# First weight loads of an expert layer: released by one memset on GpSimd in place of four on VectorE

## The chip, the cores and the metric

The kernel runs on one core of a Trainium2 chip. The metric is the device time of one execution in microseconds, the median of the runs. The engines go by the profile's names where rows are shown: PE is TensorE (PEld its weight loads), DVE is VectorE, ACT is ScalarE, POOL is GpSimd and SP is SyncE, which here only issues transfers. A small q behind a name (POOLq, SPq) is that engine's sequencer.

## The reference

A layer with a convolution gated by a query comes first, and a switch layer with eight experts after it. Only the second matters here:

```python
def _B_ref(x, w_gate, w1, w2):          # x: layernorm(h), 2048 rows of 512
    logits = xf @ w_gate                # 8 experts
    topk_idx = jnp.argsort(-logits, axis=-1)[:, :1]
    gates = _softmax(topk_val, axis=-1)
    for e in range(8):
        w = (gates * (topk_idx == e)).sum(-1, keepdims=True)
        out = out + w * (_silu(xf @ w1[e]) @ w2[e])   # w1[e]: 512 x 1792, w2[e]: 1792 x 512
h2 = h + _B_ref(_layernorm(h), ...)
```

Each token goes to one expert. All is float32.

## The kernel before

The first part (to line 611) computes the convolution and writes h, 2048 rows of 512, to a buffer in DRAM, `h_dram`. A routing part (lines 613 to 771) finds each token's expert, counts the tokens of each, picks the expert with the fewest as the first, and makes the list `idx0` of its rows. Every engine then branches on `wide_i`, a flag made from the counts, to one of three copies of `experts` (line 1037 loads it and line 1038 branches); the profiled execution takes the one with the capacities `SNUG`, in which the first expert has 240 places, two tiles of 128 and 112 rows.

Ahead of the branch, GpSimd gathers the rows of the first expert from `h_dram` in two indirect DMAs, one for each tile (line 762, tiles `rows0`, which the profile shows as part of `kt`), and SP loads the first two chunks of its weights, `raw0` (line 769). A chunk is 128x1024 numbers, 512 KB; an expert has 14, seven of w1 and seven of w2. Two memsets on GpSimd (line 781) clear `end1` and `end2`, which are used at the very end.

Inside `experts`, the order on each engine is the order in which the program writes the instructions. The float32 products are made in three passes from a high and a low part: `split_hi` copies a chunk to `whi` on ScalarE (line 877), `split_lo` subtracts on VectorE to `wlo` (line 882). `norm` (line 846, VectorE) normalises a tile of rows, `turn_x` transposes it on TensorE (line 855), copies to `xh` on ScalarE (line 856) and makes `xl` on VectorE (line 857). `up` multiplies with w1 (line 900), takes SiLU on ScalarE into one of three buffers `s` (line 903), casts to `hh` on VectorE (line 904) and subtracts to `hl` on GpSimd (line 905). `down` multiplies with w2 (lines 921 and 924). Rows of the next expert are gathered on GpSimd (line 833) while the present one is computed, and their norm and transposes stand in the middle of the present expert's `down`.

`load_w` (line 859) loads chunk s on SP: chunks 0 and 1 are `raw0`, and the following ones go to six buffers `raw` (line 869). Eight chunks are loaded ahead (`AHEAD`), and four are split ahead (`LEAD`). From chunk 8 on a load waits until `split_lo` has done with the buffer's old chunk. With `after` set, `load_w` first writes one column of the buffer, and the load has to wait for that write; the value is overwritten by the load. In the kernel before, this is done for chunks 2 to 5, on VectorE, in a place behind the norm of the first tile and a first half of `split_lo(0)`; the loads of chunks 6 and 7 stand behind them in SP's queue.

After the loads, TensorE runs through all chunks: `up` for seven, `down` for seven, expert by expert.

Of the kernel before, what the change touches and what calls it, by code (L numbers as in the profile page):

```python
# [7 lines left out]
F32 = mybir.dt.float32  # L8
# [9 lines left out]
P = 128  # L18
S, D, F, E, KS = 2048, 512, 1792, 8, 4
# [112 lines left out]
def kernel(  # L132
# [3 lines left out]
    nc = tc.nc  # L136
# [339 lines left out]
    PACE, ZERO, AHEAD = 5.404, 26.722, 1.943  # L476
# [24 lines left out]
    for n in range(ND):  # L501
        b = 4 * (n - 1)
        z, f = (b + B0, F0 * BU) if n == 0 else (b, BU)
# [37 lines left out]
        for u in range(NU):  # L541
# [11 lines left out]
            for kind, d in (("k", DA[1]), ("u", DA[2])):  # L553
                for r in range(2):
                    first = u == 0 and r == 0
# [23 lines left out]
        for u in range(NU):  # L579
            o = 4 * c + 4 + FO[c] + FS[c] * u  # L580
# [177 lines left out]
            nc.vector.tensor_reduce(perm_i, eqe, axis=AX.X, op=ALU.add)  # L758

    first = ctx.enter_context(tc.tile_pool(name="first", bufs=1))  # L760
    for t in range(2):
        nc.gpsimd.indirect_dma_start(
            out=rows0[t], out_offset=None, in_=h_dram[:, :],
            in_offset=bass.IndirectOffsetOnAxis(ap=idx0[:, t:t + 1], axis=0))
    place0 = nc.sync.value_load(least[0:1], min_val=0, max_val=E - 1)
    raw0 = []
    for ch in range(2):
        raw = first.tile([P, 1024], F32, name=f"raw{ch}")
# [7 lines left out]
    half_i = small([2], "half_i", I32)  # L776
    end = 3 * ORDER[-1] + 1
    halves = out.rearrange("s (i d) -> (s i) d", i=2)
    ends = [first.tile([P, D], F32, name="end0")] + [first.tile([P, D // 2], F32, name=f"end{i + 1}") for i in range(2)]
    for o in ends[1:]:  # L780
        nc.gpsimd.memset(o, 0.0)
    scat = []

    def scatter(to, at, o, n_rows):
# [20 lines left out]
    def experts(caps):  # L805
# [12 lines left out]
        LEAD, AHEAD = 4, 8  # L818
# [3 lines left out]
        def tiles(n):  # L822
            cap = caps[ORDER[n]]
            return [(t, r0, min(P, cap - r0), 3 * ORDER[n] + t) for t, r0 in enumerate(range(0, cap, P))]
# [34 lines left out]
        def load_w(s, after=False):  # L859
            if s >= 2 * NCH * E:  # L860
                return
            n, r = divmod(s, 2 * NCH)
            if s < len(raw0):
                PV[n], RAW[s] = place0, raw0[s]
                return
            if r == 0:
                PV[n] = nc.sync.value_load(perm_i[0:1, ORDER[n]:ORDER[n] + 1], min_val=0, max_val=E - 1)
            w, ch = (w1, r) if r < NCH else (w2, r - NCH)
            raw = RAW[s] = wp.tile([P, 1024], F32, name="raw")
            if after:  # L870
                nc.vector.memset(raw[:, 0:1], 0.0)
            nc.sync.dma_start(raw, w[bass.ds(PV[n], 1), ch].rearrange("o p f -> (o p) f"))

        def split_hi(s):
            whi = wp.tile([P, 1024], F32R, name="whi", bufs=8)
            wlo = wp.tile([P, 1024], F32R, name="wlo", bufs=8)
            nc.scalar.activation(whi, RAW[s], AF.Copy)  # L877
            W[s] = whi, wlo

        def split_lo(s, a=0, b=1024):  # L880
            whi, wlo = W[s]
            nc.vector.tensor_sub(wlo[:, a:b], RAW[s][:, a:b], whi[:, a:b].bitcast(F32))  # L882
# [80 lines left out]
                send(n, t, m, pd[:m], X["part"][:m, cols], None, ends[half + 1])  # L963

        firsts, last = tiles(0)[:-1], tiles(0)[-1]
        for s in range(len(raw0)):
            load_w(s)
            split_hi(s)
        marks(A_T, A_T, 24)
        ptab = ps_u.tile([P, 24], F32, name="acc")  # L970
        selected(ptab, A_T, 24, F16)
        norm(0, *firsts[0])
        split_lo(0, 0, 512)
        for s in range(len(raw0), AHEAD):
            load_w(s, s < 6)
        for a in firsts[1:]:
            norm(0, *a)
        for half in range(2):
# [15 lines left out]
        for s in range(2 * NCH * E):  # L994
            n, r = divmod(s, 2 * NCH)
            nx = tiles(n + 1) if n + 1 < E else []
            load_w(s + AHEAD)
            if 1 <= r - NCH < 1 + len(nx):
                norm(n + 1, *nx[r - NCH - 1])
# [38 lines left out]
    with tc.If(wide > 0, preferred_fallthrough_block=False) as sizes:  # L1038
        wider = nc.values_load(wide_i[0:1, 1:2], min_val=0, max_val=1, skip_runtime_bounds_check_because=flag)
        with tc.If(wider > 0) as more_sizes:  # L1040
            experts(CAPS)
        with more_sizes.Else():
            experts(TIGHT)
# [16 lines left out]
        with tc.If(more > 0):  # L1060
# [33 lines left out]
            for e in range(E):  # L1094
# [3 lines left out]
                with tc.For_i(min(CAPS) // P, nt) as t:  # L1098
# [29 lines left out]
                    for ch in range(NCH):  # L1128
# [3 lines left out]
                        for i in range(2):  # L1132
                            f = 2 * ch + i
                            nc.tensor.matmul(py, ht[:, f, :], wr[:, i, :], start=f == 0, stop=f == 2 * NCH - 1)
                    o = g2p.tile([P, D], F32, name="go")
# [6 lines left out]
    with sizes.Else():  # L1142
        experts(SNUG)
# [79 lines left out]
```

## Time and profile before

| | us |
|---|---|
| median of 3 runs | 543.25 (541.98 to 543.84) |
| the profiled execution, its time | 543.93 |
| its span, from the first to the last instruction | 542.0 |
| TensorE busy | 521.0 (96% of the span) |
| VectorE busy | 391.8 (72%) |
| GpSimd busy | 279.1 (52%) |
| ScalarE busy | 264.6 (49%) |

The busy times are unions over the span. Times in the rows count from the start of the span, and the stage of the change lies from about 184 to 235 us. Busy shares of the whole span say little about that stage; the timelines and the chain of waits do.

### The profile page before, as it was taken

How to read it: one execution, taken by the hardware profiler on the slowest of the kernel's cores; microseconds unless marked ns; L12 is line 12 of the kernel's file. 1: busy time of each engine (PE TensorE's matmuls, PEld its weight loads, DVE VectorE, ACT ScalarE, POOL GpSimd, SP SyncE). 2: the span in 40 equal slices, each digit the busy share in tenths (PEclk: the TensorE clock that was granted, in tenths of full speed). 3: DMA queues.
4: the chain of work that ended last, by engine and by line, in shares of the span. 5: the costliest groups of instructions: out<-in, count | busy, mean ns of one | idle time of the engine just before them, and what ended most of it. 6: DMA issues, size and time to landing. Idle time of an engine off the chain costs nothing.

```text
span 542.0 us, 12326 instructions
## 1 busy us (share of the span) xinstructions
PE 521.0 (96%) x4875; PEld 455.3 (84%) x4875; DVE 391.8 (72%) x556; ACT 264.6 (49%) x410; POOL 279.1 (52%) x324
## 2 busy tenths in 40 slices
PE   8999989999998989999999999999999999999994
PEld 8967777767656879689999999999988988988973
DVE  3779899898997979679655775864856765765851
ACT  2787887534321346545435444555544644554520
POOL 0455649865653237828703841850870850851832
PEclk9999999999999999999999999999999999999998
DMA  8919686659651378675554565665658557666401
GB/s 280 393 47 282 224 276 187 191 144 303 182 159 52 95 241 302 199 271 179 172 195 145 194 186 186 202 207 183 200 171 285 182 174 264 199 189 232 155 2 39
DMA packets 41156, 105.26 MB, mean 194 GB/s; under 512 B 5174, under 2 KB 13496, under 8 KB 40706
## 3 DMA queue, kind: packets, MB, share of 16 engines
q1 hardware_dynamic: 37682, 95.89, 53.9%
q0 software_dynamic: 3408, 8.51, 4.8%
q8 instruction: 40, 0.66, 0.5%
q14 instruction: 26, 0.21, 0.1%
HBM read 95.96 MB, written 8.50 MB: 193 GB/s over the span
## 4 chain that ended last, share of the span: by engine, by line
PE 80%; DVE 6%; issue 4%; DMA 4%; ACT 3%; POOL 1%; SPq 1%; POOLq 0%; DVEq 0%
PE acc L900 30%; PE acc L921 15%; PE acc L924 12%; PE pa L295 8%; PE pb L331 7%; PE pa L367 5%; DMA kt<-in_kt_dram 3%; PE pm L279 2%; PE pt L855 1%; DVE xa L344 1%; DVE zs L352 1%; DMA kt<-h_dram,idx 1%; PE pt L944 1%; DVE bst L381 1%; ACT ac L263 1%
## 5 line engine op out<-in xcount | busy, mean ns | idle before, releaser
L882 DVE TENSOR_TENSOR wlo<-raw,whi 128x1024 fp32r<-128x1024 f32 (+1 forms) x113 | 155.4, 1385 | 36.3 <-ACT whi L877 36.1
L905 POOL TENSOR_TENSOR hl<-s,hh 128x240 fp32r<-128x240 f32 (+5 forms) x112 | 102.8, 935 | 135.9 <-DVE hh L904 135.3
L877 ACT ACTIVATE whi<-raw 128x1024 fp32r<-128x1024 f32 x112 | 114.6, 1052 | 7.4 <-DMA raw<-in_w_dram 3.1
L903 ACT ACTIVATE s<-acc 128x240 f32<-128x240 f32 (+5 forms) x112 | 43.1, 387 | 113.0 <-PE acc L900 62.2
L904 DVE CAST hh<-s 128x240 fp32r<-128x240 f32 (+5 forms) x112 | 47.3, 430 | 54.4 <-ACT s L903 54.2
L900 PE MATMUL acc<-xh,whi 128*128 128x240 f32 (+5 forms) x448 | 72.6, 285 | 0.2 <-ACT xh L856 0.2
L900 PE MATMUL acc<-xl,whi 128*128 128x240 f32 (+5 forms) x448 | 71.8, 283 | 0.0
L900 PE MATMUL acc<-xh,wlo 128*128 128x240 f32 (+5 forms) x448 | 71.8, 283 | 0.0
L900 PEld LDWEIGHTS acc<-xh,whi 128*128 128x128 f32 x448 | 61.6, 189 | 0.9 <-ACT xh L856 0.4
L900 PEld LDWEIGHTS acc<-xl,whi 128*128 128x128 f32 x448 | 61.4, 189 | 0.0
L900 PEld LDWEIGHTS acc<-xh,wlo 128*128 128x128 f32 x448 | 61.3, 189 | 0.0
L921 PE MATMUL acc<-whi,hh 128*128 128x512 f32 (+2 forms) x136 | 54.4, 400 | 0.0
L921 PE MATMUL acc<-whi,hl 128*128 128x512 f32 (+2 forms) x136 | 53.7, 395 | 0.0
L921 PE MATMUL acc<-wlo,hh 128*128 128x512 f32 (+2 forms) x136 | 53.4, 393 | 0.0
L267 POOL TENSOR_TENSOR acc<-acc,ac 128x512 f32<-128x512 f32 x26 | 33.1, 1282 | 36.7 <-ACT acc L255 18.3
L924 PE MATMUL acc<-hh,whi 128*128 128x304 f32 (+2 forms) x168 | 49.7, 296 | 0.0
L924 PE MATMUL acc<-hl,whi 128*128 128x304 f32 (+2 forms) x168 | 49.2, 293 | 0.0
L924 PE MATMUL acc<-hh,wlo 128*128 128x304 f32 (+2 forms) x168 | 49.2, 293 | 0.0
L298 ACT ACTIVATE st<-pa 128x512 f32<-128x512 f32 x64 | 37.3, 595 | 19.6 <-PE pa L295 19.2
L295 PEld LDWEIGHTS pa<-kv,tw 128*128 128x128 f32 x256 | 30.2, 191 | 12.2 <-ACT st L298 8.7
L295 PE MATMUL pa<-kv,tw 128*128 128x128 f32 x256 | 33.5, 282 | 2.2 <-ACT st L298 2.2
L924 PEld LDWEIGHTS acc<-hh,whi 128*128 128x128 f32 x168 | 31.6, 188 | 0.1
(196 smaller groups left out, 892.4 us busy)
## 6 DMA issues: line engine op xcount, KB each, us to landing
raw<-in_w_dram SPq DMA_DIRECT2D x112, 512.0 KB, 4.2
tv<-in_tab_v_dram SPq DMA_DIRECT2D x12, 512.0 KB, 4.3
h<-in_q_dram SPq DMA_DIRECT2D x16, 256.0 KB, 5.1
kt<-in_kt_dram SPq DMA_DIRECT2D x3, 1216.0 KB, 8.0
v<-in_v_dram SPq DMA_DIRECT2D x12, 256.0 KB, 4.4
kern<-in_ssm_dram SPq DMA_DIRECT2D x12, 256.0 KB, 3.7
h<-in_x_dram SPq DMA_DIRECT2D x12, 256.0 KB, 3.5
h_dram<-h SPq DMA_DIRECT2D x12, 256.0 KB, 4.1
```

The lines of the kernel that those rows point to most:

```text
L267: nc.gpsimd.tensor_add(T[a, c, u], T[a, c, u], T[b, c, u])
L295: nc.tensor.matmul(p[:, :, j], tw[:, u * UJ + j, r, :], src[:, j, :], start=True, stop=True)
L298: nc.scalar.activation(T["s" + kind, c][:, r * NU + u], T["pa", kind, c, u, r], AF.Copy)
L331: nc.tensor.matmul(out[b, g, :], w[a], x[a, g, :], start=n == 0, stop=n == len(parts) - 1)
L877: nc.scalar.activation(whi, RAW[s], AF.Copy)
L882: nc.vector.tensor_sub(wlo[:, a:b], RAW[s][:, a:b], whi[:, a:b].bitcast(F32))
L900: nc.tensor.matmul(pu, a[:, k, at], b[:, k, :], start=i == k == 0, stop=i == 2 and k == ND - 1)
L903: nc.scalar.activation(s, pu, AF.Silu)
L904: nc.vector.tensor_copy(hh[:, f, :], s)
L905: nc.gpsimd.tensor_sub(hl[:, f, :], s, hh[:, f, :].bitcast(F32))
L921: nc.tensor.matmul(pd[:ds_.stop - ds_.start], b[:, f, ds_], a[:, f % 2, :], start=f == 0 and i == 0, stop=f == last - 1 and i == 2)
L924: nc.tensor.matmul(pd, a[:, f % 2, ds_], b[:, f, :], start=f == 0 and i == 0, stop=f == 2 * NCH - 1 and i == 2)
```

## The change

Chunks 2 to 7 are now all loaded ahead of the splits. Only the load of chunk 2 is preceded by a write to its buffer, and this write is now on GpSimd, where it stands behind the two gathers of the first expert's rows in that engine's order. Chunks 3 to 7 have no such write and follow in SP's order. The two memsets of `end1` and `end2` and the buffers themselves are moved ahead of the gathers. Nothing is computed otherwise than before.

```diff
@@ -758,6 +758,9 @@
             nc.vector.tensor_reduce(perm_i, eqe, axis=AX.X, op=ALU.add)
 
     first = ctx.enter_context(tc.tile_pool(name="first", bufs=1))
+    ends = [first.tile([P, D], F32, name="end0")] + [first.tile([P, D // 2], F32, name=f"end{i + 1}") for i in range(2)]
+    for o in ends[1:]:
+        nc.gpsimd.memset(o, 0.0)
     for t in range(2):
         nc.gpsimd.indirect_dma_start(
             out=rows0[t], out_offset=None, in_=h_dram[:, :],
@@ -776,9 +779,6 @@
     half_i = small([2], "half_i", I32)
     end = 3 * ORDER[-1] + 1
     halves = out.rearrange("s (i d) -> (s i) d", i=2)
-    ends = [first.tile([P, D], F32, name="end0")] + [first.tile([P, D // 2], F32, name=f"end{i + 1}") for i in range(2)]
-    for o in ends[1:]:
-        nc.gpsimd.memset(o, 0.0)
     scat = []
 
     def scatter(to, at, o, n_rows):
@@ -868,7 +868,7 @@
             w, ch = (w1, r) if r < NCH else (w2, r - NCH)
             raw = RAW[s] = wp.tile([P, 1024], F32, name="raw")
             if after:
-                nc.vector.memset(raw[:, 0:1], 0.0)
+                nc.gpsimd.memset(raw[:, 0:1], 0.0)
             nc.sync.dma_start(raw, w[bass.ds(PV[n], 1), ch].rearrange("o p f -> (o p) f"))
 
         def split_hi(s):
@@ -963,16 +963,15 @@
                 send(n, t, m, pd[:m], X["part"][:m, cols], None, ends[half + 1])
 
         firsts, last = tiles(0)[:-1], tiles(0)[-1]
+        for s in range(AHEAD):
+            load_w(s, s == len(raw0))
         for s in range(len(raw0)):
-            load_w(s)
             split_hi(s)
         marks(A_T, A_T, 24)
         ptab = ps_u.tile([P, 24], F32, name="acc")
         selected(ptab, A_T, 24, F16)
         norm(0, *firsts[0])
         split_lo(0, 0, 512)
-        for s in range(len(raw0), AHEAD):
-            load_w(s, s < 6)
         for a in firsts[1:]:
             norm(0, *a)
         for half in range(2):
```

## Rows read from the trace of the kernel before

**Rows 1.** This is the profile's page, its part in 40 equal slices of the span: the TensorE clock that was granted, in tenths of full speed.

```profile
PEclk9999999999999999999999999999999999999998
```

**Rows 2.** This is the timeline of TensorE, 184 to 236 us: start, duration, line, operation, tiles, shapes, count, and in brackets the idle time ahead of it and what ended that.

```profile
194.56 0.63 PE L855 MATMUL pt<-cs,xr 128*128 128x128 f32 x4 [1.50 <-DVE xr L846]
...
196.50 1.19 PE L900 MATMUL acc<-xh,whi 128*128 128x240 f32 x8 [0.22 <-ACT xh L856]
...
226.55 0.66 PE L855 MATMUL pt<-cs,xr 128*128 128x128 f32 x4 [1.14 <-DVE xr L846]
```

**Rows 3.** This is busy time by stretches: start and end, length, then for each engine the busy time and the number of instructions, the granted clock of TensorE, the DMA engines' share, GB/s.

```profile
196.50:225.40 28.90, 28.90 (x210) 26.46 (x210) 21.75 (x36) 15.13 (x27) 19.62 (x23) 1.00 0.85 290
...
226.60:533.50 306.90, 306.90 (x2171) 288.08 (x2172) 204.29 (x251) 143.79 (x226) 151.79 (x149) 1.00 0.56 186
...
538.00:540.00 2.00, 0.00 (x0) 0.00 (x0) 0.00 (x0) 0.00 (x0) 0.00 (x0) 0.50 0.01 2
```

**Rows 4.** This is the chain of waits from 184 to 232 us: start, duration, what.

```profile
189.51 4.33 DMA kt<-h_dram,idx
...
195.19 0.67 PE acc L985 x6
...
196.50 19.20 PE acc L900 x168
...
226.00 0.51 DVE xr L846
```

**Rows 5.** This is the timeline of VectorE, 184 to 232 us, columns as in rows 2.

```profile
195.07 0.06 DVE L871 MEMSET raw<- 128x1 f32 x1
195.07 0.41 DVE L846 TENSOR_SCALAR xr<-kt,mr 112x256 f32<-112x256 f32 x1
...
202.71 1.25 DVE L882 TENSOR_TENSOR wlo<-raw,whi 128x1024 fp32r<-128x1024 f32 x1 [0.74 <-ACT whi L877]
204.37 1.23 DVE L882 TENSOR_TENSOR wlo<-raw,whi 128x1024 fp32r<-128x1024 f32 x1 [0.42 <-ACT whi L877]
205.51 0.47 DVE L904 CAST hh<-s 128x240 fp32r<-128x240 f32 x2
...
224.81 1.23 DVE L882 TENSOR_TENSOR wlo<-raw,whi 128x1024 fp32r<-128x1024 f32 x1 [0.58 <-ACT whi L877]
```

**Rows 6.** This is the timeline of ScalarE, 182 to 232 us, columns as in rows 2.

```profile
201.61 1.06 ACT L877 ACTIVATE whi<-raw 128x1024 fp32r<-128x1024 f32 x1 [1.81 <-DMA raw<-in_w_dram]
203.28 1.06 ACT L877 ACTIVATE whi<-raw 128x1024 fp32r<-128x1024 f32 x1 [0.61 <-DMA raw<-in_w_dram]
...
207.72 0.37 ACT L903 ACTIVATE s<-acc 128x240 f32<-128x240 f32 x1 [1.65 <-POOL hl L905]
...
223.46 0.37 ACT L903 ACTIVATE s<-acc 128x240 f32<-128x240 f32 x1 [2.59 <-POOL hl L905]
223.73 3.89 ACT L877 ACTIVATE whi<-raw 128x1024 fp32r<-128x1024 f32 x4
```

**Rows 7.** This is the timeline of GpSimd, 182 to 245 us, columns as in rows 2.

```profile
189.51 1.20 POOL L762 DMA_INDIRECT kt<-h_dram,idx  x1 [1.73 <-DVE wide_i L736]
191.01 0.95 POOL L762 DMA_INDIRECT kt<-h_dram,idx  x1 [0.30 <-issue]
191.96 0.58 POOL L781 MEMSET end<- 128x256 f32 x2
...
205.88 3.89 POOL L905 TENSOR_TENSOR hl<-s,hh 128x240 fp32r<-128x240 f32 x4 [1.88 <-DVE hh L904]
...
218.55 1.37 POOL L905 TENSOR_TENSOR hl<-s,hh 128x240 fp32r<-128x240 f32 x2
...
222.72 1.37 POOL L905 TENSOR_TENSOR hl<-s,hh 128x240 fp32r<-128x240 f32 x2
```

**Rows 8.** This is the instructions of line 1038 (the branch on wide_i) from 189 to 192 us, one on each sequencer: count, shortest, median and longest duration in ns, first and last start in us.

```profile
L1038 POOLq COMPARE_BRANCH  x1: 40/40/40, 190.2 to 190.2; - x1
L1038 SPq COMPARE_BRANCH  x1: 53/53/53, 190.7 to 190.7; - x1
```

**Rows 9.** This is what SP's DMA queue waited for, 190 to 200 us: the line, what ended the wait, us in total, times, the longest.

```profile
SPq L872 <- DVE xr L846: 4.5, 1, 4.5
```

**Rows 10.** This is busy time by stretches around the gathers of the first expert, and one where the gathers of the next one run; columns as in rows 3.

```profile
192.50:193.00 0.50, 0.50 (x9) 0.46 (x8) 0.00 (x0) 0.50 (x1) 0.04 (x1) 1.00 0.56 123
...
193.50:194.00 0.50, 0.00 (x0) 0.00 (x0) 0.13 (x1) 0.00 (x0) 0.00 (x0) 1.00 0.70 270
...
194.50:195.00 0.50, 0.44 (x4) 0.47 (x5) 0.50 (x1) 0.00 (x0) 0.00 (x0) 1.00 0.00 0
...
195.50:196.00 0.50, 0.50 (x7) 0.48 (x6) 0.50 (x2) 0.32 (x1) 0.00 (x0) 1.00 0.00 0
196.00:196.50 0.50, 0.28 (x4) 0.07 (x2) 0.50 (x2) 0.41 (x2) 0.00 (x0) 1.00 0.63 131
196.50:197.00 0.50, 0.50 (x4) 0.50 (x5) 0.50 (x2) 0.28 (x2) 0.00 (x0) 1.00 0.95 270
...
217.00:218.00 1.00, 1.00 (x6) 0.80 (x5) 0.70 (x2) 0.00 (x0) 0.69 (x2) 1.00 0.84 266
```

**Rows 11.** This is DMA issues by line in the stretch 190.95 to 191.5 us, which holds the second gather of the first expert alone: count, and the median us from issue to landing.

```profile
kt<-h_dram,idx POOLq DMA_INDIRECT x1, 3.8
```

**Rows 12.** This is the same for 216.1 to 217.3 us, which holds the first gather of the next expert alone.

```profile
hr<-h_dram,idxg POOLq DMA_INDIRECT x1, 5.6
```

## The prediction

> **What bounds the kernel now.** I read the page first. TensorE's granted clock stays at its upper level until the last slice [rows 1], and the engine is busy for 521 of 542 us. So only its own idle time can be given back, and the next view is its timeline, with the idle time ahead of an instruction in brackets: transposes of normalised rows waited 1.50 us for VectorE's norm at 194.56 and 1.14 at 226.55, and the first matmul of the experts 0.22 for a ScalarE copy [rows 2]. By stretches, TensorE has no gap from 196.5 to 225.4 and none from 226.6 to 533.5 [rows 3]. The expert phase therefore has two weak places: the wait for the first rows ahead of 196.5, and one hole from 226.55 - 1.14 = 225.41 on.
>
> The chain of waits says how the first comes about [rows 4]. The first gather is issued at 189.51 and lands 4.33 later, norm, transposes, three warming matmuls (195.19 + 0.67 = 195.86), ScalarE's copy, and the first matmul at 196.50. The weights for it (raw 0 and 1) are loaded elsewhere and the edit leaves them alone. So the six loads that are moved are not on this chain.
>
> The second place hangs on GpSimd. The hole ends when VectorE has done the norm for expert 1 (226.00 + 0.51) [rows 4]. Going back from there: VectorE's split of chunk 11 at 224.81 [rows 5] waits for ScalarE's copy at 223.73, which stands behind a SiLU copy at 223.46 that waited 2.59 us for GpSimd's hl (three buffers of s) [rows 6]. GpSimd runs from 205.88 to that hl at 222.72 with hl and the gathers of expert 1 [rows 7]. It starts at 205.88 because VectorE casts the first hh only at 205.51, after the splits of chunks 2, 3 and 4; two of these were preceded by idle time, 0.74 and 0.42 us, both for ScalarE [rows 5], and ScalarE had waited 1.81 and 0.61 us for the landing of raw [rows 6]. Thus late weights do reach TensorE, by a long way round.
>
> **The change part by part.** *The wait removed.* SP was through its branch at 190.7 and then stood 4.5 us before the first of the six loads, at 195.17 [rows 8, 9]. GpSimd's sequencer was through its branch at 190.2 [rows 8], so its memset of 128x1 can run right behind the second gather, whose issue ends at 191.01 + 0.95 = 191.96, as the memsets of 128x256 do now [rows 7]. A 128x1 memset on GpSimd isn't in the trace: below it is nothing, above it is one of 128x256, 0.33 us (two in 0.58, overlapped). I take 0.2. The loads then leave at about 192.2, 3.0 us earlier. Behind the waiting instruction on SP are only loads 3 to 7 and the ones that wait for their buffers.
>
> *What the earlier loads give.* The idle 0.74 + 0.42 on VectorE goes, since chunks 3 and 4, which ScalarE began at their landing at 201.61 and 203.28 [rows 6], then land some 3 us earlier, before VectorE comes to them. The four VectorE memsets went together at 195.07 and the next norm started at the same 195.07 [rows 5]; I put 0.05 on them (nothing to the 0.06 of the one that shows by itself). VectorE's lead at the first hh is 1.16 + 0.05 = 1.21 us. I carry it one to one along GpSimd's queue to the norm at 226.00, since the outputs of TensorE lie waiting: the SiLU copy of 207.72 also waited for hl, not for TensorE [rows 6].
>
> *The memsets of ends.* They move ahead of the two gathers, 0.58 us. GpSimd stood 1.73 us before the first gather [rows 7], which hides them; without that cover the whole 0.58 would be on the chain, at the gather. Cost: nothing. The three fewer memsets, and the loads written ahead of the splits, add nothing to any other queue.
>
> *What the earlier loads cost.* The second gather is still moving. The first load, issued at 195.17, moves nothing until 196.0 [rows 10], so one issued at 192.2 starts near 193.15. The gather's data run from 192.9 to 194.5 (123 to 270 GB/s, gone by 194.5) and nothing else is in the queues [rows 10]; its tail of 1.3 us would be shared. The price g, by which the second gather lands later: nothing, if the engines have room; above, the gather of expert 1 that was issued amid loads (DMA share 0.84 [rows 10]) took 5.6 us to land where this one took 3.8, so 1.8 [rows 11, 12]. I take 0.9, half, because here the gather has a start of 0.3 us and a load moves at half rate in its first half microsecond (131 GB/s, then 270 [rows 10]): 1.8 x (1.3 - 0.5) / 1.6 = 0.9.
>
> With g, the second tile's norm (195.07, its data there since 191.01 + 3.8 = 194.8) has a slack of 0.2, and TensorE, which is at the warming matmuls until 195.86 while the first half is ready at 195.48, another 0.4. So VectorE's lead is 1.21 - (g - 0.2), and TensorE starts g - 0.6 late. At 226.55 TensorE resumes at the later of 226.55 minus the lead and 225.41 plus the late start. g = 0.9: lead 0.51, start 0.3 late, gain 0.5. g = 0: the whole 1.14. g = 1.8: lead -0.39, a loss of 0.4.
>
> **The sum.** Gain 0.5 us (1.14 to -0.4). The profiled execution took 543.93 us (span 542.0 and 1.93 around it), 0.68 above the median of 543.25. It would take 543.4; a median of like runs 543.25 - 0.5 = 542.75, said as 542.7.
>
> The Trainium skill has a rule that speaks against this change (*DMA: Bandwidth & Descriptors*, *Queues, rings and completion order*): each DMA engine goes round robin, a packet at a time, between the queues that have work. By that rule the gather's data could at most take twice their 1.6 us, g up to 1.6 and a loss of 0.2 where the row gives up to 0.4; it leaves no place for the third rival below. The longer landing amid loads [rows 12] agrees with it.
>
> **The rivals.**
> 1. *No contention, the hole closes.* Gain 1.14: 542.1. For it: a DMA share of only 0.56 to 0.70 under the gather [rows 10]. Against it: 5.6 against 3.8 us [rows 11, 12].
> 2. *The loads leave earlier and nothing comes of it.* Either the memset is held on GpSimd, or the lead is eaten on the way: VectorE's splits and GpSimd's hl run side by side, and the four hl from 205.88 took 3.89 us where two took 1.37 later [rows 7]. Gain 0: 543.25. This is also the case that the change doesn't do what it says; against it, the branch at 190.2 [rows 8].
> 3. *Slower: the gather is held behind the loads.* The place is the second tile's norm. Six loads stand in SP's queue; two that followed each other landed 203.28 - 201.61 = 1.67 us apart [rows 6]. If the gather's rest comes only after two of them, g = 3.3, and the loss is 3.3 - 0.2 - 1.21 = 1.9: 545.2. It decides from g = 1.4 on (no gain) and is beyond a measurement of this kernel from g = 3.0 on. TensorE would then stand for over 4 us, and after it stops at 534 its granted clock is at 0.50, the lower of its two levels, by 538 [rows 3]; such a fall would come on top. Against it: even amid loads a gather landed within 5.6 us.
> 4. *More than the hole.* Faster by over 1.6 us would need idle time of TensorE that isn't there, other than the 1.5 us for the first gather, whose data are through before the loads start.
>
> **How the numbers follow.** About 0.3% (1.6 us) is what a measurement of this kernel can tell from no change; its three runs alone span 541.98 to 543.84. Forecast (542.7, contention in part): 0.60. Rival 1 (542.1): 0.15. Rival 2 (543.25): 0.12. Rival 3 (545.2): 0.08. Rival 4: 0.05. Of the first three, 0.87 together, I give 0.08 to medians that fall below 541.6 by spread alone and 0.01 to ones above: faster 0.13, same 0.78, slower 0.09. The range is 542.1 to 543.65 from the bounds of g, with the spread of the medians, about 0.9 below and 0.3 above: 541.2 to 543.9.
>
> **What would show it.** After: the first of the six loads issued at 192.0 to 192.4, behind a memset at 191.96; the second gather landing 0.2 to 1.6 us later than 3.8 from its issue; first matmul at 196.5 to 197; no idle time on VectorE before the splits of chunks 3 and 4; the first hl near 205.4; the hole at 225.4 down from 1.14 to a few tenths. Wrong if the first matmul is later than 197.5, or the hole stays at 1.1 with the loads early, or a hole opens that isn't in the trace of before.

## The result, and the profile after

The changed kernel is slower: a median of 546.8 us (544.17 to 547.77, 9 runs) against 543.62 before (541.98 to 544.08, 9 runs), a ratio of 1.006 with a 95% interval of 1.004 to 1.008. Its profiled execution took 547.41 us with a span of 545.6, 3.6 longer than the span before.

What TensorE waited for from 186 to 534 us (line, what ended the wait, us in total, times, the longest), after:

```profile
PE acc L855 <- DVE xr L846: 2.2, 1, 2.2
PE pt L855 <- DVE xr L846: 0.4, 1, 0.4
```

The hole ahead of the next expert's transposes, 1.14 us in [rows 2], is gone. In its place stand 2.2 us at the transposes of the second tile (tile acc), which had no wait before. The chain of waits, 180 to 240 us, after:

```profile
190.78 6.47 DMA kt<-h_dram,idx
...
197.28 0.42 DVE xr L846
...
198.89 21.45 PE acc L900 x168
220.34 9.72 PE acc L921 x42
```

The second gather now stands on the chain, where the first stood before [rows 4]: 6.47 us from issue to landing instead of 3.8 [rows 11]. The first matmul is at 198.89 and not at 196.50, and its group of 168 takes 21.45 us and not 19.20. The granted clock, in stretches (columns as in rows 3), after:

```profile
196.50:197.00 0.50, 0.00 (x0) 0.00 (x0) 0.00 (x0) 0.00 (x0) 0.00 (x0) 1.00 0.95 246
197.00:198.85 1.85, 0.98 (x4) 0.63 (x4) 1.57 (x4) 0.36 (x1) 0.00 (x0) 0.51 0.89 308
198.85:204.00 5.15, 5.11 (x24) 5.11 (x25) 4.94 (x13) 3.64 (x6) 1.03 (x2) 0.51 0.77 311
204.00:220.00 16.00, 16.00 (x145) 16.00 (x144) 13.05 (x19) 7.78 (x15) 14.00 (x16) 1.00 0.72 238
```

TensorE has no instruction at 196.5 to 197.0, the clock falls to its lower level, and the first 24 matmuls take 5.1 us. The standing in TensorE's timeline, after:

```profile
194.77 0.83 PE L984 MATMUL acc<-cs 128*128 128x128 f32 x6
197.84 0.98 PE L855 MATMUL acc<-cs,xr 112*128 112x112 f32 x4 [2.23 <-DVE xr L846]
```

TensorE ran out of work at 194.77 + 0.83 = 195.60, and the clock fell at 197.0, 1.4 us into the standing. The account of the span: 198.89 - 196.50 = 2.39 for the late start, 21.45 - 19.20 = 2.25 for the clock, less 1.14 for the hole, together 3.50 of the 3.6 us.

What released the loads: GpSimd's and SP's timelines, after.

```profile
190.78 0.95 POOL L765 DMA_INDIRECT kt<-h_dram,idx  x1 [0.30 <-issue]
191.73 0.12 POOL L871 MEMSET raw<- 128x1 f32 x1
```

```profile
191.87 3.94 SPq L872 DMA_DIRECT2D raw<-in_w_dram  x6
```

The first load is issued 0.14 us after the gather's issue has ended (190.78 + 0.95 = 191.73). DMA packets by queue in 194.7 to 197.1 us, after (packets, MB, share of 16 engines):

```profile
q1 hardware_dynamic: 210, 0.75, 93.6%
q0 software_dynamic: 4, 0.01, 1.3%
```

Queue 0 carries the gathers, queue 1 the loads. Before, neither gathers nor loads moved from 194.5 on until the first load's data at 196.0 [rows 10]. Now a last four of the gather's packets come in this stretch among 210 of the loads, and the norm of 112 rows waits for them. The two gathers of the first expert are 160 packets of queue 0, 80 each, so it is a small part of the second gather that comes last.

### The profile page after: what moved, and what is told of

Its sections match the earlier page's. It is cut to its first block, busy times and chain, and to the rows that moved or that the text cites. A ratio compares the mean times of both kernels' runs of the same rounds, so it can differ in the third digit from the quotient of the medians.

```text
span 545.6 us, 12320 instructions
## 1 busy us (share of the span) xinstructions
PE 524.8 (96%) x4875; PEld 458.5 (84%) x4875; DVE 390.8 (72%) x552; ACT 264.4 (48%) x410; POOL 277.5 (51%) x325
## 4 chain that ended last, share of the span: by engine, by line
PE 82%; DVE 8%; issue 4%; DMA 2%; ACT 2%; POOL 1%; POOLq 0%; DVEq 0%
PE acc L900 30%; PE acc L921 15%; PE acc L924 12%; PE pa L295 8%; PE pb L331 7%; PE pa L367 4%; PE pa L459 2%; DVE xa L344 2%; PE pm L279 2%; PE pt L855 1%; DMA kt<-h_dram,idx 1%; DVE zs L352 1%; DVE p L340 1%; PE pt L944 1%; DVE bst L381 1%
## 5 line engine op out<-in xcount | busy, mean ns | idle before, releaser
L905 POOL TENSOR_TENSOR hl<-s,hh 128x240 fp32r<-128x240 f32 (+5 forms) x112 | 100.4, 914 | 138.2 <-DVE hh L904 137.7
```

What stands on the lines that cost most here:

```text
L905: nc.gpsimd.tensor_sub(hl[:, f, :], s, hh[:, f, :].bitcast(F32))
```

## The experiments

Theory A, made from this: the loads run beside the end of the second gather, it lands late, TensorE stands, and standing lowers its clock. Medians of the kernel before, measured together with each version, stand beside its result.

**Which part of the change.** `rest` puts the release back (the one memset on VectorE again, and the loads in their old place in the program) and leaves all else; `landed` keeps the place and makes the loads wait for the gather's landing.

```diff
 # rest: the loads of chunks 2 to 7 again behind split_lo(0, 0, 512)
-                nc.gpsimd.memset(raw[:, 0:1], 0.0)
+                nc.vector.memset(raw[:, 0:1], 0.0)
 ...
-        for s in range(AHEAD):
-            load_w(s, s == len(raw0))
+        for s in range(len(raw0)):
+            load_w(s)
 ...
         split_lo(0, 0, 512)
+        for s in range(len(raw0), AHEAD):
+            load_w(s, s == len(raw0))
 # landed
-                nc.gpsimd.memset(raw[:, 0:1], 0.0)
+                nc.gpsimd.tensor_copy(raw[:, 0:1], rows0[1][:, 0:1])
```

Expected of rest: 

> The changed kernel without the early release: the one memset is on VectorE again, behind the norm of the first tile; the rest of the change (one memset, not four; the memsets of ends ahead of the gathers; the buffers) stays. Theory A: the second gather lands after 3.8 us, the first matmul at 196.4, time 543.2 to 544.0, the same as before. Theory B: 546 to 547.

Expected of landed: 

> The changed kernel, but the write to chunk 2's buffer on GpSimd copies one column of the second gather's rows, so the loads wait until that gather has landed. Theory A (the six loads share the DMA engines with the second gather, it lands late, TensorE stands and its clock falls): the gather lands 3.8 us after its issue as before, the first load is issued near 194.8, the first matmul of the experts is at 196.2 to 196.6 at the upper clock, and the time is 543.0 to 543.8. Theory B (the loss comes from another part of the change: the buffers that lie elsewhere, the memsets of ends ahead of the gathers, the loads written ahead of the splits): the time stays at 546 to 547.

Measured: rest 543.85 us, ratio 1.0004 [0.9991, 1.0017]; landed 543.83, ratio 1.0005 [0.9991, 1.0020]; before 543.35. Theory B falls: the buffers that lie elsewhere, the single memset, the memsets of ends in their new place and the order of the loads cost nothing that these runs can tell. The loss is in the early release.

**The clock.** `warm` fills TensorE's time, `idle` makes TensorE stand without any early load.

```diff
 # warm, on the changed kernel
-        for _ in range(3):
+        for _ in range(12):
             nc.tensor.matmul(warm, const("one"), cs[:, :P], start=True, stop=True)
 # idle, on rest
+        for _ in range(4):
+            nc.vector.memset(ends[0], 0.0)
         for half in range(2):
             norm(0, *last, half)
```

Expected of warm: 

> The changed kernel with twelve warming matmuls in place of three between the transposes of the two tiles, so that TensorE is busy while the second gather is late. Theory A: the gather is as late as in the changed kernel (6 to 6.5 us from issue), the first matmul is still near 198.9, but the granted clock stays at its upper level, the first 168 matmuls take 19.2 us and not 21.45, and the time is 544.2 to 544.9. Theory C (the clock falls for another reason than TensorE's standing, such as the DMA traffic or where the stage happens to lie): the clock falls all the same and the time is 546.5 or more.

Expected of idle: 

> The kernel of the run rest (one memset on VectorE in the old place, so that no load is early) with four memsets of 128x512 on VectorE ahead of the norm of the second tile: about 2.2 us more of standing for TensorE, without any transfer beside the second gather. Theory A: standing alone lowers the clock. The gather lands 3.8 us after issue, the first matmul is near 198.7, part of the first 168 matmuls runs at the lower level, and the time is 545.0 to 547.0. Theory C (the clock fell because of the transfers, not because TensorE stood): the clock stays up and the time is 544.0 to 544.7, the late start less the hole of 1.1 us.

Measured: warm 544.4 us, ratio 1.0026 [1.0013, 1.0040], before 543.35; idle 547.37, ratio 1.0056 [1.0031, 1.0082], before 543.44. VectorE's timeline of warm (norm of the second tile), then TensorE's stretches of warm:

```profile
196.54 0.74 DVE L846 TENSOR_SCALAR xr<-kt,mr 112x256 f32<-112x256 f32 x2 [2.15 <-DMA kt<-h_dram,idx]
```

```profile
193.00:198.10 5.10, 4.88 (x49) 4.46 (x47) 2.80 (x6) 0.98 (x3) 0.00 (x0) 1.00 0.95 331
198.10:217.10 19.00, 18.97 (x168) 18.97 (x169) 17.97 (x30) 11.41 (x21) 12.96 (x15) 1.00 0.77 260
```

The gather is late here too (VectorE waits 2.15 us for it), but TensorE is busy meanwhile, the clock stays up and the 168 matmuls take 19.0 us. The median is 2.4 us below that of the changed kernel, which agrees with the 2.25 of its trace. Nor do transfers alone lower the clock: the DMA engines are 95% busy in the first of these stretches. TensorE's waits in idle, its stretches, a line of its chain, and the landing of its second gather in the stretch 191.9 to 195:

```profile
195.08 0.63 PE L855 MATMUL pt<-cs,xr 128*128 128x128 f32 x4 [1.63 <-DVE xr L846]
195.54 0.83 PE L988 MATMUL acc<-cs 128*128 128x128 f32 x6
198.46 0.98 PE L855 MATMUL acc<-cs,xr 112*128 112x112 f32 x4 [2.08 <-DVE xr L846]
```

```profile
196.60:203.40 6.80, 4.87 (x22) 4.55 (x23) 6.28 (x17) 2.90 (x6) 0.00 (x0) 0.50 0.92 329
203.50:220.00 16.50, 16.50 (x149) 16.50 (x149) 14.87 (x20) 9.12 (x17) 14.22 (x16) 1.00 0.79 276
```

```profile
199.51 20.88 PE acc L900 x168
```

```profile
kt<-h_dram,idx POOLq DMA_INDIRECT x1, 3.9
```

With the gather on time and TensorE standing, the clock is at its lower level for 6.8 us and the time is about that of the changed kernel. The account is the same too: 199.51 - 196.50 = 3.0 for the late start, 20.88 - 19.20 = 1.7 for the clock, less 1.14 for the hole, 3.6 in all, as the spans differ (545.6 and 542.0). The median lies above the range of theory A, and further above the 544.0 to 544.7 of theory C, which falls as far as it put the clock down to transfers: neither an early load nor a late gather is needed for this loss.

Which standing lowered the clock in idle is not shown. TensorE ran out of work at 195.54 + 0.83 = 196.37, and the clock was down from 196.6 on, 0.2 us into the added standing; another of 1.63 us had ended at 195.08. And standing isn't the only thing that the clock falls after. A stretch of rest, all that TensorE waited for in rest from 186 to 534 us, and a stretch of the changed kernel ahead of its gathers' landing:

```profile
191.60:198.30 6.70, 6.42 (x35) 4.81 (x35) 4.65 (x12) 2.88 (x6) 0.95 (x1) 0.50 0.62 193
```

```profile
PE pt L855 <- DVE xr L846: 0.2, 1, 0.2
```

```profile
192.00:192.50 0.50, 0.50 (x2) 0.02 (x1) 0.00 (x0) 0.23 (x1) 0.00 (x0) 0.50 0.57 229
```

In rest the clock was down from 191.6 to 198.3 with TensorE busy before and in it, and in the changed kernel it was down once already while TensorE ran the matmuls ahead of the first transposes. There it cost little: the first transposes came at 194.30 in the changed kernel and at 194.56 before [rows 2], and the median of rest is that of before. Why it fell there is open. What warm shows is narrower than theory A: with the gather late, keeping TensorE busy at this place kept the clock up.

**How many loads, and how early.** `early1` releases chunk 2 alone on GpSimd, the others from VectorE in the old place; `early1_again` is the same kernel; `nowait` drops the memset.

```diff
 # early1
-                nc.gpsimd.memset(raw[:, 0:1], 0.0)
+                (nc.gpsimd if s == len(raw0) else nc.vector).memset(raw[:, 0:1], 0.0)
 ...
-        for s in range(AHEAD):
+        for s in range(len(raw0) + 1):
             load_w(s, s == len(raw0))
 ...
         split_lo(0, 0, 512)
+        for s in range(len(raw0) + 1, AHEAD):
+            load_w(s, s == len(raw0) + 1)
 # nowait
-            load_w(s, s == len(raw0))
+            load_w(s)
```

Expected of early1: 

> Only chunk 2 is released early, by the memset on GpSimd; chunks 3 to 7 wait for a memset on VectorE in the old place. Theory A, with a price that grows with the bytes beside the gather: one load of 512 KB is 1.3 us of traffic, the gather lands 4.3 to 5.0 us after issue, the first matmul is at 196.5 to 197.2, time 543.0 to 544.3. Theory D (one packet of the gather on one DMA engine is held up as soon as any load is beside it): the gather is as late as with six loads, 6 us and more, and the time is 546 or more.

Expected of early1_again: 

> The same kernel as early1, for a second profile. Its runs lay apart, 542.7 to 544.4 and 545.5 to 546.2, and the profiled one was late (546.23, gather 6.1 us). If a late gather is an event of some executions, a profile near 543.5 shows the second gather landing 3.8 to 4.5 us after issue; one near 546 shows 5.5 us or more again.

Expected of nowait: 

> The changed kernel without its memset: the six loads leave as soon as SP is through its branch, near 190.9, before the second gather is issued, and move from 191.9 on, beside both gathers. Theory A (the price grows with the bytes beside the gathers): the first gather lands later too, by 0.5 to 1.5 us, the second 2.7 us late or more, the first matmul at 199.5 or later, and the time is 547 to 550. Theory D (one DMA engine's share of the gather is held up, however many loads there are): the second gather 2 to 3 us late as in the changed kernel, 546 to 547.5.

Measured: early1 543.85 us, ratio 1.0003 [0.9984, 1.0022], before 543.35, runs from 542.7 to 546.23; early1_again 544.21, ratio 1.0010 [0.9992, 1.0028], before 543.52, runs from 542.15 to 546.21; nowait 547.9, ratio 1.0078 [1.0059, 1.0098], before 543.52. The norm of the second tile on VectorE in early1, and in early1_again:

```profile
197.22 0.74 DVE L846 TENSOR_SCALAR xr<-kt,mr 112x256 f32<-112x256 f32 x2 [1.81 <-DMA kt<-h_dram,idx]
```

```profile
195.26 0.73 DVE L846 TENSOR_SCALAR xr<-kt,mr 112x256 f32<-112x256 f32 x2 [1.07 <-DMA kt<-h_dram,idx]
```

Their second gathers on GpSimd:

```profile
191.16 0.95 POOL L765 DMA_INDIRECT kt<-h_dram,idx  x1 [0.30 <-issue]
```

```profile
190.81 0.95 POOL L765 DMA_INDIRECT kt<-h_dram,idx  x1 [0.30 <-issue]
```

The gathers were issued at 191.16 and 190.81, so the norm came 6.06 and 4.45 us later, in one and the same kernel with one load released beside the gather. Queue 0 (the gathers) from 194.8 to 197.0 us in early1, and in early1_again, and a stretch of early1 in the columns of rows 3:

```profile
q0 software_dynamic: 5, 0.02, 1.8%
```

```profile
q0 software_dynamic: 1, 0.00, 0.0%
```

```profile
195.50:196.00 0.50, 0.50 (x4) 0.50 (x3) 0.00 (x0) 0.18 (x1) 0.00 (x0) 0.50 0.19 74
```

In the late execution 5 packets of the gather's 80 were still to come, a sixteenth of it, and this while the DMA engines were only 19% busy. The next load was issued at 195.5, behind VectorE's memset, so the one early load had delayed the gather before any other left. The price is thus not a fixed one for so many bytes: a single load can do what six do, and need not. Theory D is right that a small part of the gather is held up and that one load is enough, and wrong that it happens each time. The first expectation of early1 held for the median and failed for the profile, which was taken of the slowest of the ten executions. VectorE in nowait, and its queue 0 from 194.8 to 198.5 us:

```profile
193.76 0.55 DVE L846 TENSOR_SCALAR xr<-kt,mr 128x512 f32<-128x512 f32 x1 [1.30 <-DMA kt<-h_dram,idx]
...
199.01 0.74 DVE L846 TENSOR_SCALAR xr<-kt,mr 112x256 f32<-112x256 f32 x2 [4.00 <-DMA kt<-h_dram,idx]
```

```profile
q0 software_dynamic: 75, 0.24, 18.1%
```

The gathers' issues on GpSimd and the loads' on SP, in nowait:

```profile
190.19 1.19 POOL L765 DMA_INDIRECT kt<-h_dram,idx  x1 [1.23 <-DVE wide_i L736]
191.68 0.95 POOL L765 DMA_INDIRECT kt<-h_dram,idx  x1 [0.30 <-issue]
```

```profile
191.66 4.01 SPq L872 DMA_DIRECT2D raw<-in_w_dram  x6
```

Here the loads were issued at 191.66, 0.97 us ahead of the end of the second gather's issue (191.68 + 0.95), and its norm came 7.33 us after issue; 75 of its 80 packets came late, not only the last few. The first gather, whose issue had ended 0.28 us ahead of the first load, was not late (issued at 190.19, norm 3.57 later), against what theory A expected of it, while the time lies in theory A's range of 547 to 550.

**How late is late enough.** `later` puts four memsets between the gather and the release; `ends_behind` undoes one part, the move of the two memsets of ends.

```diff
 # later, in load_w
+                for _ in range(4):
+                    nc.gpsimd.memset(ends[1], 0.0)
                 nc.gpsimd.memset(raw[:, 0:1], 0.0)
 # ends_behind
-    for o in ends[1:]:
-        nc.gpsimd.memset(o, 0.0)
     for t in range(2):
         nc.gpsimd.indirect_dma_start(
 ...
+    for o in ends[1:]:
+        nc.gpsimd.memset(o, 0.0)
     place0 = nc.sync.value_load(least[0:1], min_val=0, max_val=E - 1)
```

Expected of later: 

> The changed kernel with four memsets of 128x256 on GpSimd between the second gather and the memset that releases the loads: the release comes 1.0 to 1.3 us later, near 192.9, and the first load moves from 193.8 on, when most of the gather's data are through. Theory A: the gather lands 3.8 to 4.6 us after issue, first matmul 196.3 to 196.9, time 542.8 to 544.0. Theory D (any load beside the end of the gather holds one DMA engine's share up): 6 us and more in the profile, and a time of 545 or more, or a spread of the runs as wide as with one early load.

Expected of ends_behind: 

> The changed kernel with the two memsets of ends in their old place, behind the second gather: the release comes 0.5 to 0.6 us later than in the changed kernel, 0.6 to 0.8 us after the end of the gather's issue, between the 0.14 of the changed kernel (gather 5.6 to 6.5 us) and the 1.5 of the run later (3.5 us). Theory A, with a price that grows with the gather's data that are still to move: the gather lands 4.2 to 5.2 us after issue, the time is 543.3 to 545.5. If only loads that start before the gather's first data do harm: 3.8 us and 542.8 to 543.5. If any load beside the tail does harm: 5.5 us and more, 546 to 547.

Measured: later 542.95 us (541.47 to 543.97), ratio 0.9989 [0.9976, 1.0003], before 543.44; ends_behind 542.26, eight of ten runs from 541.7 to 542.95 and two at 545.12 and 545.61, ratio 0.9990 [0.9971, 1.0008], before 543.47. GpSimd of ends_behind, and VectorE of ends_behind:

```profile
190.57 0.95 POOL L763 DMA_INDIRECT kt<-h_dram,idx  x1 [0.30 <-DVE mr L742]
191.52 0.58 POOL L767 MEMSET end<- 128x256 f32 x2
192.02 0.11 POOL L871 MEMSET raw<- 128x1 f32 x1
```

```profile
194.42 0.73 DVE L846 TENSOR_SCALAR xr<-kt,mr 112x256 f32<-112x256 f32 x2 [0.48 <-DMA kt<-h_dram,idx]
...
203.58 0.47 DVE L904 CAST hh<-s 128x240 fp32r<-128x240 f32 x2
```

With the two memsets behind the gather the first load is issued at 192.16, 0.64 us after the gather's issue has ended and not 0.14, and the norm comes 3.85 us after the gather's issue: half a microsecond decides between this profile and that of the changed kernel and, by the runs, in most executions. The median lies below all three ranges written down for it, nearest to the second possibility (only loads ahead of the gather's first data do harm). The two runs at 545 may mean that 0.64 is not always enough; they have no profile, and of 31 runs of the kernel before two were at 545.36 and 547.02 as well. In later, with 1.50, no run of ten was above 544. VectorE of later, and TensorE's waits of later:

```profile
195.20 0.73 DVE L846 TENSOR_SCALAR xr<-kt,mr 112x256 f32<-112x256 f32 x2
...
204.35 0.47 DVE L906 CAST hh<-s 128x240 fp32r<-128x240 f32 x2
```

```profile
PE pt L855 <- DVE xr L846: 0.3, 1, 0.3
PE acc L902 <- ACT xh L856: 0.2, 1, 0.2
```

The second norm doesn't wait for its gather, the first hh is cast at 204.35 where it was at 205.51 [rows 5], and the hole at 225 is gone.

**The hole, and a faster version.** `s_bufs` gives s five buffers in the kernel before, `landed_s` in landed. `best` is later with five buffers and six warming matmuls ahead of the first transposes.

```diff
-                s = xp.tile([P, cap], F32, name="s", bufs=3)
+                s = xp.tile([P, cap], F32, name="s", bufs=5)
```

Expected of s_bufs: 

> The kernel before with five buffers of s in place of three, and nothing else. If the hole at 225.4 hangs on ScalarE waiting for a buffer of s behind GpSimd, as the prediction had it, VectorE's norm for the next expert is ready in time, the hole of 1.14 us closes and the time is 542.0 to 542.8, against 543.4 before. If the norm waits for something else, the hole stays and the time is 543.0 to 543.8.

Expected of landed_s: 

> The kernel of the run landed (loads wait for the landing of the second gather) with five buffers of s. Theory A: the gather is undisturbed and the hole closes, 542.0 to 542.8. If the hole hangs on something else: 543.4 to 544.0, as landed was.

Expected of best: 

> The kernel of the run later, with five buffers of s and six warming matmuls of 128 columns ahead of the first transposes. Theory A: the loads leave at 193.9 and the gather is undisturbed; the standing of 1.5 us ahead of the transposes is nearly filled, so the clock falls less often in this stage; and the hole at 225 is closed. 541.5 to 542.7 against 543.4 before. If the clock of this stage is set by what came before the gathers, the six matmuls bring nothing and it is 542.7 to 543.2, as later.

Measured: s_bufs 543.37 us, ratio 0.9989 [0.9973, 1.0005], before 543.44; landed_s 542.94, ratio 0.9994 [0.9980, 1.0007], before 543.44; best 543.4, ratio 0.9996 [0.9986, 1.0006], before 543.52. VectorE and then the granted clock of s_bufs:

```profile
223.48 0.72 DVE L846 TENSOR_SCALAR xr<-hr,rec 128x512 f32<-128x512 f32 x1 [1.16 <-DMA rec<-rec_dram,idxg]
```

```profile
195.20:198.50 3.30, 3.23 (x17) 2.88 (x15) 2.80 (x11) 1.39 (x4) 0.00 (x0) 0.50 0.58 211
```

The norm for the next expert came at 226.00 before [rows 4], and is 2.5 us earlier now and ends its wait on a transfer: the hole did hang on the buffers of s. But the gain doesn't show in the time beyond its interval: all three medians lie above the ranges written for a closed hole. In this execution the clock fell at the start of the stage, with no early load at all. No version here is faster than the kernel before beyond the uncertainty; later and ends_behind come nearest. In the profile of best the clock stays at 1.00 from 190 to 217, and its median is still that of before, so filling the standing ahead of the first transposes is not shown to bring anything.

## Why the prediction was wrong

The range was 541.2 to 543.9 and the sign was that of a small gain.

- *The wait removed.* Right: the memset ran right behind the gather, 0.12 us long (0.2 taken), and the first load left at 191.87, 3.3 us earlier than 195.17 (0.23 of it since the gather was issued at 190.78 and not at 191.01).
- *What the earlier loads give.* Right in size: from the second norm to the first hh cast it took 205.51 - 195.07 = 10.44 us before, 206.41 - 197.28 = 9.13 after and 204.35 - 195.20 = 9.15 in later. The lead is 1.3 us, where 1.21 was worked out, and with the gather on time it closes the hole.
- *What the earlier loads cost.* This is the step that failed. g was taken as 0.9 between nothing and 1.8; it was 6.47 - 3.8 = 2.7 in the changed kernel, and 7.33 less 3.8, 3.5, in nowait. The row taken as the upper end, a gather amid loads at 5.6 us [rows 12], was one instance of a wait that differs from execution to execution (6.06 and 4.45 us for one kernel), so it bounded nothing. The trace of before held a second instance, the gather of expert 1 issued at 220.1, with the DMA share at 0.83:

  ```profile
  DMA to landing us min/median/max: 3.7/3.7/3.7
  ```

  Between 3.7 and 5.6 amid loads, the row was a draw from a spread and no upper end. The reasoning by shares of the queue, 1.8 x (1.3 - 0.5) / 1.6, sized the mean slowing of the packets, while the norm waits for the last one: 4 packets of queue 0 among 210 of queue 1 came at the very end. The rule cited there from the Trainium skill (*DMA: Bandwidth & Descriptors*, *Queues, rings and completion order*) was worked out to at most 1.6; 2.7 and 3.5 were measured, and the measurement decides: taking turns by packets was no bound for the landing. That section of the Trainium skill lets an engine drain a whole packet of several descriptors before it turns to another queue and does not say that the packets of two queues hold equal data, so "at most twice" did not follow from it. The sign written for being wrong, a first matmul later than 197.5, came true with 198.89.
- *The clock.* The sum had no term for it. It was written under the third rival, on top of a standing of over 4 us; here it fell 1.4 us into a standing of 2.23 us, and it cost 2.25 us, nearly as much as the late start. The 4 us were too long as well: nowait, with g at 3.5, stood 3.29 us.
- *The memsets of ends* were put at nothing, since GpSimd's wait hides them in their new place. That is right for the place they went to, and misses the place they left: behind the gather their 0.58 us would have held the loads back, and with them there (ends_behind) eight of ten runs are at 541.7 to 542.95. This was the other half of the failure.
- *The rivals.* The third was the right mechanism at the right place, at 0.08. With its own formula, g = 2.7 gives 2.7 - 0.2 - 1.21 = 1.3 us of loss; with the clock's 2.25 that makes 3.5, near the 3.6 of the spans. That the formula fits is in part luck: it goes by VectorE's norm at the hole, while in the trace the hole is gone and the loss is TensorE's late start, 2.39 - 1.14 = 1.25.

What stays open is why the last few packets of the gather are held, and why in some executions and not in others. That they were a sixteenth of it in early1, with 16 DMA engines, fits one engine that comes late with its share; but the views here don't tell the engines apart, and no run changed it on one engine alone, so this is not shown. Open too is what lowers the clock while TensorE is busy, as in rest.

## What to carry to other kernels

A transfer that a stage waits for is priced by its last packet, not by its share of bandwidth: a load that is released right behind it can cost more than it brings, and half a microsecond between them decided here. A write that seems to do nothing but take time behind a transfer may be what keeps the next transfers off it, so a step that is moved has a price where it leaves too. And where TensorE would stand, cost the clock with the standing: in the changed kernel each was worth over 2 us.

## What the runs showed of the hardware that was not expected

- With one load of 512 KB issued 0.14 us after the end of a 256 KB gather's issue, the norm came 6.06 us after the gather's issue in one execution, with 5 of the gather's 80 packets last, and 4.45 in another. With six loads issued 0.64 us after, it came after 3.85; without loads the gather landed after 3.8.
- With no transfer late, the granted clock was at 0.50 from 196.6 to 203.4 after standings of 1.63 us and 0.2 us of one of 2.08 (idle). It goes by the execution: before, TensorE stood 1.50 us ahead of 194.56 [rows 2] and the clock was 1.00 right after, and in s_bufs, with 1.6 us at the same place, it was 0.50 from 195.2 to 198.5.
- The clock also fell with TensorE at work: in rest it was at 0.50 from 191.6 to 198.3, where TensorE's only wait was 0.2 us, and the median was that of before.
